# An attention and expert kernel with idle products at its start, seven logits, narrower scatters and new sequences

## The chip, the cores and the metric

The kernel runs on one core of a Trainium2 chip. The metric is the device time of one execution in microseconds. In the profile PE is TensorE, PEld its weight loads, DVE is VectorE, ACT is ScalarE, POOL is GpSimd and SP is SyncE, whose queue issues nearly all DMAs.

## The reference

Four batches of 12288 tokens of 128 numbers attend to 768 keys, which are means over 4 x 4 patches of `kv` times a matrix. What comes out goes, token by token, to the one of eight experts that has the largest logit.

```python
kv_pool = kv.reshape(B, H // r, r, W // r, r, C).mean(axis=(2, 4))
kv_flat = kv_pool.reshape(B, -1, C) @ w_sr
k = v = kv_flat
a = softmax(q @ k.transpose(0, 2, 1) / sqrt(C))      # rows of 768
x = (a @ v).reshape(B * N, C)
logits = x @ w_gate                                  # 8 experts
expert_idx = argmax(logits, axis=1)
gate_w = softmax(logits)[arange(N), expert_idx]
y = relu(x @ w1[expert_idx]) @ w2[expert_idx]        # 128 -> 1024 -> 128
out = gate_w[:, None] * y
```

## The kernel before

The tokens are worked on in 96 blocks of 512, 24 to a batch. For each batch `keys` first sums patches: twelve loads of `kv` are added in pairs on DVE (L604), and PE sums the rest and turns it by products with a unit matrix (`ident`), eight to a pair of loads. Projections with `w_sr` follow, then `expert` fetches the weights of the expert that the batch's mean points to, orders its hidden units and keeps 384 of them. The permutations that do this are written by comparisons (`PU`, L960).

A block computes scores (`s`) of 512 queries against six tiles of 128 keys, subtracts the exponential (ACT, `e`) from its linear part (DVE, `r`), and multiplies `r` with a tile of values: 24 products, four chunks of tokens by six tiles of keys, `XW` = 145 columns wide, to which a correction of 136 columns is added three times for each chunk. The columns behind the first 128 hold eight logits, the row sum, and eight sums over bands of keys by which tokens that lie badly are found. A first-guess expert serves all tokens of a batch. `group` and `marks` compare the logits, and tokens for which the guess fails are listed. A `general_step` per batch (three of them inside the schedule, after batches 0 to 2) fetches such tokens' values, works them out with their own expert and writes them over the results by a scatter on POOL (L1674). What is left over then goes through a loop at the end.

A block's hidden units come in three parts of 128. The third part has a flag by block (the ways named `u`): with it a sum is taken along by ACT and PE leaves out the last four products of that block; the blocks 14, 22, 37, 39 and 95 had no such flag.

The order is not left to a compiler. Each piece of work is an `op` of a class `Plan`, with engine, estimated time, what it needs and gives, and buffers. A table `ORDER` gives each engine its own sequence, a table `WAYS` picks between forms of a piece, and `order` walks both and starts what can start first. PSUM has two banks of the kind `b`, two double banks `s` and one `po`. Where PE would stand still in given stretches of the planner's time, the planner puts in idle products (`fill`): three products of 128 by 384 of the constant `slots16`, into a bank `b` that nobody reads. The constants are written by DVE and POOL ahead of the plan, in a schedule of their own.

Of the kernel before, what the change touches and what calls it, by code (L numbers as in the profile page):

```python
# [9 lines left out]
F32 = mybir.dt.float32  # L10
F16 = mybir.dt.float16
# [73 lines left out]
PE 0-2 4-5 3 6-7 9-10 8 11 112 13 114 12 100 16 101 115 14 113 103 15 147 17-18 102 23 119 117 146 118 116 19 105 148 104  # L85
107 106 125 124 151 150 149 126 152 135 24 136 26 20 129-130 128 137 127 157 25 31 159 141 139-140 138 21 158 32 168 22 169
161 160 162-163 30 170 28 181 27 29 180 121 173 179 120 172 174 171 108 191 131-132 190 185 182-183 192 122 184 123 133 212
201 195 110 134 109 203 194 153 193 155 196 154 202 111 213 142 214 206 143 207 223 164 205 224 204 33 144 236 145 225 216
165 218 217 234 215 34 186 235 156 245 227 188 187 229 226 228 246-247 208 166 238 240 239 237 257 175 35 258 248-249 36 256
197 189 251 176 268 177 250 37 267 167 178 262 269 260 198 259 209 261 278 199 210 280 270 200 272 220 273 279 219 271 211  # L90
39 291 283 290 282 231 281 284 221 289 230 38 300 222 301 40 42 41 294 232 293 292 302 241 295 313 243 233 312 252 304 242
306 253 311 46 305 324 263 303 47 323 43 317 48 244 322 265 314 316 315 254-255 49 333 328 326 264 276 327 335 44 274 325
334 275 266 346 285 344 45 339 287 337 345 307 277 355 286 336 338 296 298 357 356 297 350 348-349 347 381 288 380 308 360
309 361 359 401 358 299 52 390 379 50 53 392 318 383 403 385 329 402 319 382 51 384 391 310 412 406 320 407 413 330 321 414
362 404 341 405 331 425 340 332 423 393 363 396 364 395 394 424 343 415 418 435 417 416 434 386 351 436 426-427 429 54 428
445 55 365 352 446 438 342 439 447 437 387 366 440 456 397 388 458 449 353 450 457 448 451 354 469 467 398 389 408 468 461
399 419 479 460 367 459 410 462 409 480 430 400 478 421 473 470-472 420 500 411 501 56 482 431 57 370 483 452 489 432 491
# [4 lines left out]
591 600 70 612 593 66 532 611 553 610 71 602-603 605 551 604 552 72 622 621 562 543 613 623 614 632 563-564 616 615 554 633  # L102
573 634 565 67 656 575 626-627 624 574 625 658 68 657 584 636 638 667 585 635 637 576 689 76 668 662 659 586 661 660 595 691
669 75 73 587 596 690 671 607 673 672 670 606 712 617 74 695 678 597-598 680 693 608 679 692 619 694 700 639 609 701 683 618
682 702 628 684 630 681 629 713 620 722 703 641 640 705-706 711 77 643 734 704 78 631 724 642 723 675 714 716-717 664 715
663 733 665 735 674 685 725 727 644 726 745 676 728 666 744 687 737 739 746 738 707 696 736 677 766 747 697-698 768 749 748
686 750 767 718 79 647 699 778 645 777 770 80 769 646 709 779 771 729 772 708 688 719 757 756 782 720 710 783 755 731 780
648 781 649 730 789 760 759 721 650 741 790 758 761 788 651 799 740 654 801 652 791 800 732 793-794 792 810 751 81 811 802
82 804 812 773 753 803 805 653 834 83 833 742 815 813 752 814 743 821 774 816 822 655 823 762 832 754 775 843 824 784 826
844 763 85 827 845 825 776 84 856 835 855 786 838 837 86 854 764 836 88 87 846 785 848 867 849 795 847 765 866 92 876 858  # L110
796 860 797 857 859 865 787 798 877 888 808 93 806 819 89 807 868 878 871 869-870 818 887 817 889 94 881 880 809 900 879 95
898 882 840 820 893 899 829 892 90 828 891 890 91 830 911 910 839 850 904 831 933 901 903 852 934 902 842 97 909 935 841 96
98 956 912 862 913 851 915 914 99 863 944 957 936 853 861 938 955 883 939 872 937 946 873 864 894 966 874 961 884 945 875
# [8 lines left out]
1063 1147 1106 1165 1167 1116 1064 1180 1117 1179 1154 1181 1118 1108 1182 1138 1128 1153 1155 1119 1170 1129 1168 1127 1150
1169 1171 1183 1190 1151 1188 1149 1130 1156-1157 1140 1159 1139 1189 1152 1164 1158 1174 1141 1184 1192 1185 1194 1172-1173
1191 1193 1186-1187 1175 1160 1195 1161-1162 1197 1196 1200 1198 1163 1199 1201
ACT 0 2 1 3-4 6 5 7 113 9 115 8 104 10 105 116 11 114 107 12-13 139 20 19 14-15 106 138 117-118 140 108 123 109 122 22 124
130 21 142 141 23 131 16-17 132 18 125 146 126 24 148 29 133 147 154 30 155 149 28 156 150 26 164 25 134 27 163 120 162 119
158 157 110 172 128 171 127 173 121 165-166 129 185 112 178 111 180 167 143 145 174 179 144 186 135 187 136 193 151 194 31
181 204 137 195 152 202 32 189 188 203 168 210 170 169 196-197 212 211 153 182 206 205 218 33 219 159 34 217 175 198 160-161
# [226 lines left out]
def attention_moe(ctx: ExitStack, tc, q, kv, w_sr, w_gate, w1, w2, out):  # L355
# [43 lines left out]
    with tc.manual_schedule():  # L399
# [68 lines left out]
        for t in con:  # L468
            nc.vector.memset(t, 0.0)
# [1282 lines left out]
```

## Time and profile before

| | us |
|---|---|
| median of three runs | 727.38 |
| lowest and highest run | 727.12, 729.40 |
| the profiled execution's own time | 728.98 |
| its span | 727.2 |
| PE busy | 695.8 |
| DVE busy | 632.3 |
| ACT busy | 609.2 |
| POOL busy | 538.4 |

The span counts from the first to the last instruction; 1.78 us of the profiled execution lie around it. Busy times are those of the engine itself; register, branch and DMA-issuing instructions are not counted. The times in the views below are from the start of that span. The chain that ended last is followed from the last instruction back, at each step to what released it or to the instruction ahead of it on its engine.

### The profile page before, as it was taken

The page shows a single profiled execution, that of the slowest core. Times are in us where ns is not written, and L with a number is a line of the kernel's source. Part 1 is how long each engine was busy: PE and PEld are TensorE (multiplying, and loading weights), DVE is VectorE, ACT ScalarE, POOL GpSimd, SP SyncE. Part 2 cuts the span into 40 slices and gives each one's busy share as a digit, 9 for nine tenths or more (in the row PEclk, how much of TensorE's full clock was granted, in tenths as well). Part 3 has the DMA queues.
Part 4 walks back from the last instruction along what each step waited for, and adds up shares of the span by engine and source line. Part 5 has one row for each costly group of instructions (what it writes and reads, how often), then busy time and mean ns, then how long its engine had stood idle before and what let it go on. Part 6 is the DMA issues. An engine that isn't in the chain of part 4 may idle for free.

```text
span 727.2 us, 20777 instructions
## 1 busy us (share of the span) xinstructions
PE 695.8 (96%) x7874; PEld 548.7 (75%) x7874; DVE 632.3 (87%) x1262; ACT 609.2 (84%) x1120; POOL 538.4 (74%) x770
## 2 busy tenths in 40 slices
PE   4998999999999999999999999999999999999995
PEld 4676777888778767887687777888877877877774
DVE  5789888889998989789999898898998899778875
ACT  0578899899898988889878888899988898898973
POOL 0455899886888879686778978888778778657643
PEclk9999999999999999999999999999999999999999
DMA  8795987995999999878999999879886798985842
GB/s 336 186 271 116 248 200 185 196 211 127 202 250 243 229 232 216 198 175 136 184 211 209 230 218 275 167 146 211 156 170 152 175 186 195 195 154 117 130 91 74
DMA packets 324389, 138.25 MB, mean 190 GB/s; under 512 B 210190, under 2 KB 315794, under 8 KB 324288
## 3 DMA queue, kind: packets, MB, share of 16 engines
q1 hardware_dynamic: 323536, 136.55, 85.6%
q8 instruction: 62, 1.02, 0.6%
q14 instruction: 39, 0.32, 0.1%
q10 hardware_dynamic: 560, 0.20, 0.1%
q0 software_dynamic: 192, 0.17, 0.1%
HBM read 59.12 MB, written 26.94 MB: 118 GB/s over the span
## 4 chain that ended last, share of the span: by engine, by line
PE 71%; DVE 13%; ACT 7%; issue 4%; DMA 3%; POOL 1%; SPq 0%; DVEq 0%; ACTq 0%; POOLq 0%
PE b L478 31%; PE po L478 22%; PE s L478 16%; DVE r L1189 6%; ACT e L1187 3%; DMA kv<-in_kv_dram 2%; DVE y L1318 1%; DMA x<-xp 1%; ACT g L1293 1%; ACT X L1281 1%; DVE xp L1224 1%; ACT xp L1223 0%; DVE junk L1428 0%; PE s L859 0%; PE s L1588 0%
## 5 line engine op out<-in xcount | busy, mean ns | idle before, releaser
L1189 DVE SCALAR_TENSOR_TENSOR r<-s,e 128x1024 bf16<-128x1024 f32 x288 | 346.4, 1216 | 34.9 <-ACT e L1187 33.0
L1187 ACT ACTIVATE e<-s 128x1024 f32<-128x1024 f32 x288 | 294.2, 1031 | 35.6 <-PE s L478 29.8
L478 PE MATMUL po<-v,r 128*128 128x145 f16 x2304 | 252.9, 227 | 1.0 <-ACT lg L1231 0.8
L478 PEld LDWEIGHTS <-r 128*128 128x128 bf16 x2304 | 167.7, 98 | 21.6 <-DVE xp L1224 1.3
L478 PE MATMUL s<-qT,KT 128*128 128x512 f16 x576 | 168.0, 379 | 2.4 <-DVE r L1189 1.4
L478 PE MATMUL b<-x,w1U 128*128 128x512 f16 x465 | 142.5, 379 | 5.0 <-DMA x<-xp 1.5
L1293 ACT ACTIVATE g<-b,zb 128x512 f16<-128x512 f32 x187 | 129.3, 694 | 11.5 <-PE b L478 10.9
L478 PE MATMUL po<-M,qT 128*128 128x136 f16 x1152 | 130.9, 223 | 0.0
L1285 POOL TENSOR_TENSOR g<-X,g 80x512 f16<-80x512 f32 x94 | 108.8, 1157 | 29.1 <-ACT g L1293 9.5
L478 PE MATMUL b<-w2U,g 128*128 128x128 f16 x1172 | 128.3, 219 | 1.3 <-POOL g L1285 1.3
L478 PE MATMUL b<-L,x 128*128 128x128 f16 x1116 | 122.9, 219 | 0.1
L1170 POOL TENSOR_TENSOR qp<-qr,qp 128x512 f16<-128x512 f32 x94 | 108.8, 1160 | 8.5 <-DVE w1l L1012 1.2
L478 PEld LDWEIGHTS <-qT 128*128 128x128 f16 x1152 | 84.5, 98 | 28.1 <-issue 3.1
L478 PEld LDWEIGHTS <-x 128*128 128x128 f16 x1116 | 80.8, 98 | 16.8 <-issue 3.2
L1168 POOL CAST qp<-qr 128x512 f16<-128x512 f32 x94 | 57.2, 613 | 41.2 <-DMA qr<-in_q_dram 21.1
L1283 POOL CAST g<-X 128x512 f16<-128x512 f32 x94 | 58.2, 620 | 36.3 <-ACT X L1281 18.3
L478 PEld LDWEIGHTS <-g 128*128 128x128 f16 x1172 | 81.6, 98 | 1.4 <-POOL g L1285 1.4
L619 POOL TENSOR_TENSOR kv<-kv,kv 128x512 f32<-128x512 f32 x54 | 68.2, 1273 | 12.8 <-DVE sg L873 2.2
L478 PEld LDWEIGHTS <-w1U 128*128 128x128 f16 x480 | 45.7, 98 | 38.2 <-issue 4.2
L1281 ACT ACTIVATE X<-b,zb 128x512 f32<-128x512 f32 x94 | 65.1, 696 | 9.6 <-PE b L478 9.5
L1318 DVE TENSOR_TENSOR y<-b,gt 128x512 f32<-128x512 f32 (+1 forms) x97 | 65.3, 676 | 6.8 <-PE b L478 5.0
L478 PEld LDWEIGHTS <-KT 128*128 128x128 bf16 x576 | 51.0, 99 | 25.7 <-issue 4.6
(386 smaller groups left out, 912.0 us busy)
## 6 DMA issues: line engine op xcount, KB each, us to landing
qr<-in_q_dram SPq DMA_DIRECT2D x96, 256.0 KB, 3.6
out_dram<-y SPq DMA_DIRECT2D x95, 256.0 KB, 3.3
kv<-in_kv_dram SPq DMA_DIRECT2D x41, 512.0 KB, 6.0
raw<-in_moe_w_dram SPq DMA_DIRECT2D x14, 512.0 KB, 5.5
e<-in_kv_dram SPq DMA_DIRECT2D x3, 512.0 KB, 8.8
v_dram<-vT SPq DMA_DIRECT2D x4, 384.0 KB, 3.9
qT<-qp SPq DMA_TRANSPOSE x94, 3.7
x<-xp SPq DMA_TRANSPOSE x91, 3.6
```

The costliest lines, as they stand in the source:

```text
L478: return nc.tensor.matmul(o, l, r, start=start, stop=stop)
L619: nc.gpsimd.tensor_add(flat(to), flat(to), flat(of))
L1168: op("POOL", .62, lambda: nc.gpsimd.tensor_copy(qp.tile[:, 0], qr.tile), T - 1.9 * LEN, [("qr", t)], [("qh", t)], [qr, qp])
L1170: op("POOL", 1.17, lambda: nc.gpsimd.tensor_sub(qp.tile[:, 1], qr.tile, qp.tile[:, 0]), T - 1.8 * LEN, [("qh", t)], [("qp", t)], [qr, qp])
L1187: op("ACT", 1.03, lambda e=e, ps=ps: nc.scalar.activation(e.tile, ps.tile, AF.Exp), at + .6, [("s", t, s)], [("e", t, s)], [ps, e])
L1189: op("DVE", 1.22, lambda e=e, ps=ps, s=s: nc.vector.scalar_tensor_tensor(r.tile[:, 2 * s:2 * s + 2], ps.tile, 1.0, e.tile, op0=ALU.add, op ...
L1224: op("DVE", .69, lambda: nc.vector.tensor_tensor(xp.tile[:, 1], po.tile[:, :, :C], xp.tile[:, 0], op=ALU.subtract), A + .5, [("xh", t)], [ ...
L1281: op("ACT", .69, lambda ph=ph, zu=zu: nc.scalar.activation(gf.tile, ph.tile, AF.Relu, bias=zu()), at + .5, [("ph", t, u), ("zb", b)], [("g ...
L1283: op("POOL", .62, lambda: nc.gpsimd.tensor_copy(gg.tile[:, 0], gf.tile), at + 1.5, [("gf", t)], [("gh", t), ("g", t)], [gf, gg])
L1285: op("POOL", 1.16, lambda: nc.gpsimd.tensor_sub(gg.tile[:PAIRS, 1], gf.tile[:PAIRS], gg.tile[:PAIRS, 0]), at + 2, [("gf", t), ("gh", t), ( ...
L1293: op("ACT", .78, lambda u=u, ph=ph, zu=zu: nc.scalar.activation(gg.tile[:, u], ph.tile, AF.Relu, bias=zu(), accum_out=k["fl"].tile[:, u - ...
L1318: nc.vector.tensor_tensor(y.tile[:, cs], py.tile.rearrange("p (c d) -> p c d", d=C)[:, cs], bc(gr["gt"].tile[:, 0, js], C)[:, cs], op=ALU. ...
```

## The change

- The logit of the first-guess expert is no longer carried: seven others (`EO = E - 1`) stand in the extra columns. `XW` becomes 144 and the correction 135 columns. `relative` and a new step `others` fill the gap with the eighth expert.
- The blocks 14, 37 and 39 take the way with a flag.
- The scatter of a general step names only the rows of the batches that are done (12288, 24576 and 36864 instead of 49152), and `v_dram` likewise.
- The two loads of expert weights in a general step are an operation of their own; in `expert` they are two.
- Idle products are allowed from 3.5 instead of 9.0 us of the planner's time. Their groups of three go from 11 to 20: 11 ahead of the first key sums, one among them and 8 later. Before, all 11 came after the key sums.
- Constants and plan share one schedule.
- `ORDER` and `WAYS` are new: twelve of the 32 `PU` rows are written by POOL, tiles of `kt` and the first scaled weights leave DVE, and 18 instead of 20 blocks send `x` over POOL. Some new forms are written but not picked (`f`, `n`, `y`).

```diff
-PE 0-2 4-5 3 6-7 9-10 8 11 112 13 114 12 100 16 101 115 14 113 103 15 147 17-18 102 23 119 117 146 118 116 19 105 148 104
...
-            if o.eng == "PE" and any(lo < free["PE"] and start < hi for lo, hi in self.filler_times):
+            spans = [lo for lo, hi in self.filler_times if lo < start and free["PE"] < hi] if o.eng == "PE" else ()
+            if spans:
                 make, fill, us = self.filler
+                free["PE"] = max(free["PE"], spans[0])
...
-    XW = C + NG + 1 + E
+    EO = E - 1
+    XW = C + EO + 1 + NG
...
-    with tc.manual_schedule():
-        ident = keep("ident", [P, P])
...
+    written = ExitStack()
+    written.enter_context(tc.manual_schedule())
+    ident = keep("ident", [P, P])
...
-        op("DVE", .8, unit, at + 2, [("pd", b), ("mean", b)], [("unit", b)], [pd])
+        op("DVE", .87, unit, at + 2, [("pd", b), ("mean", b)], [("unit", b)], [pd])
...
+            op("ACT", .2 + .21 * w, lambda sl=sl: nc.scalar.activation(
+                kt.tile[:, sl], vT.tile[:, sl], AF.Identity, bias=cn[:, :1], scale=cn[:, 4:5]), at + 2.1 + n,
+               [("unit", b), ("vT", b)], [("kt", b), ("kt", b, n)], [vT, kt], way=(f"t{b}{n}", 1))
...
+        def others():
+            c = cg.tile
+            nc.vector.scalar_tensor_tensor(c[:, 0, :EO], c[:, 1, :EO], c[:, 0, EO:], c[:, 0, :EO], op0=ALU.mult, op1=ALU.add)
+            nc.vector.tensor_scalar(c[:, 4, 1:2], cn[:, 12:13], -1.0, -1.0, op0=ALU.mult, op1=ALU.add)
+            nc.vector.scalar_tensor_tensor(c[:, 2, :EO], c[:, 1, :EO], c[:, 4, 1:2], iota_e[:, :EO], op0=ALU.mult, op1=ALU.add)
...
+        op("DVE", .7, others, at + 12, [("cg", b)], [("off", b)], [cg], lock=True)
...
+            if way:
+                op("POOL", .5, lambda j=j: nc.gpsimd.tensor_scalar(
+                    PU.tile[:, j], slots16, sg.tile[:, 8, j:j + 1], 1.0, op0=ALU.is_equal, op1=ALU.mult),
+                   at + 22 + j / 2, [("odd", b)], [("perm", b, j)], [PU, sg], way=(way, 1))
...
-                            mm(po.tile[:, c, :P + E], own_q(c, i), M.tile[:, j], False, False)
...
+                            mm(po.tile[:, c, :P + EO], own_q(c, i), M.tile[:, j], False, False)
...
-        part("SP", 2.3, load, ["find"], "load", [gi, vT, *raw], 4.5, moves=4.2)
+        part("SP", 1.1, load, ["find"], "load", [gi, vT], 4.0, moves=1.0)
+        part("SP", 1.6, load_w, ["find"], "loadw", [gi, *raw], 4.5, moves=3.4)
...
-            out=out, out_offset=bass.IndirectOffsetOnAxis(ap=li(4), axis=0),
-            in_=o.tile, in_offset=None, bounds_check=B * N - 1, oob_is_err=False), ["o"], "done", [gi, o], 2.5)
+            out=out[:upto * N], out_offset=bass.IndirectOffsetOnAxis(ap=li(4), axis=0),
+            in_=o.tile, in_offset=None, bounds_check=upto * N - 1, oob_is_err=False), ["o"], "done", [gi, o], 2.5)
...
-            op("DVE", .8, count_steps, START + (t + 5) * LEN + 3, [("left", b)], [("steps", b)], lock=True)
+            op("DVE", .8, count_steps, START + (t + 5) * LEN + 3,
+               [("left", b)] + [("general", b - 1, "find2")] * (b - 1 in STEPS_AFTER), [("steps", b)], lock=True)
...
-    plan.filler, plan.filler_times = (bank().make, fill, .487), ((9.0, 110.0), (690.0, 800.0))
-    with tc.manual_schedule():
-        plan.issue()
+    plan.filler, plan.filler_times = (bank().make, fill, .487), ((3.5, 110.0), (690.0, 800.0))
+    plan.issue()
+    written.close()
```

On PE the program began with the product of the gate weights' maximum (`b0_166`) and the first key sums; a name is the tile with a running number, behind it the operands and the shape, and in brackets the engines waited for.

```order
L478 MATMUL b0_166<-wg_st_95,ones_72 128x1 [waits DVE_49]
L478 MATMUL s0_208<-ident_65,kv3_176 128x128 [waits DVE_49,Pool_49]
L478 MATMUL s0_208<-ident_65,kv3_176 128x128 x7
L478 MATMUL s0_208<-ident_65,kv2_174 128x128 x8
L478 MATMUL s1_226<-ident_65,kv4_180 128x128 [waits DVE_49]
```

Now the idle groups stand between them; the first, the second and the last of the eleven:

```order
L483 MATMUL b0_161<-wg_st_95,ones_72 128x1 [waits DVE_49]
L483 LDWEIGHTS slots16_86
L483 MATMUL b1_194<-slots16_86 128x384
...
L483 MATMUL b1_198<-slots16_86 128x384 [waits PE_49]
...
L483 MATMUL b1_234<-slots16_86 128x384 [waits PE_49]
...
L483 MATMUL s0_238<-ident_65,kv2_167 128x128 [waits DVE_49,Pool_49]
L483 MATMUL s0_238<-ident_65,kv2_167 128x128 x7
```

All eleven groups go to the bank `b1`, and each but the first waits for PE itself, for the group ahead of it in that bank; `b0_161` holds the other bank.

On DVE the reduction of the gate weights (L514, now L519) was the first instruction, and the last constants stood among the key additions:

```order
L514 TENSOR_REDUCE wg_st<-wg_raw 128x1
L403 CAST ident_h<-ident 128x128
...
L452 TENSOR_SCALAR band_i<-part_i 128x1
L604 TENSOR_TENSOR kv_174<-kv_174,kv_164 128x1024
L453 CAST band<-band_i 128x1
L604 TENSOR_TENSOR kv_176<-kv_176,kv_172 128x1024
```

Now it is behind all of them:

```order
L470 MEMSET ends 128x65
L474 MEMSET con_143 128x32
...
L519 TENSOR_REDUCE wg_st<-wg_raw 128x1
L609 TENSOR_TENSOR kv_167<-kv_167,kv_165 128x1024
L609 TENSOR_TENSOR kv_169<-kv_169,kv_163 128x1024
L486 TENSOR_SCALAR wg_st<-b_161 128x1
```

All constants have moved ahead of the reduction, and the reader of the product of the gate weights (L486) behind two key additions.

On POOL the scatter of the first general step stood ahead of casts and subtractions of hidden units, and waited for two DMA queues:

```order
L995 TENSOR_SCALAR sg_6038<-sg_6038,ws_6196 128x8 [waits Pool_49]
L1674 DMA out_dram<-pool_5680,gi_4611 49152x128 [waits DMAHW5_49,DMAHW0_49]
L1283 CAST g_6086<-X_6265 128x512 [waits Activation_49]
L1229 TENSOR_TENSOR xp_6182<-X_6148,xp_6182 128x512 [waits DVE_49]
L1283 CAST g_6185<-X_6164 128x512 [waits PE_49]
L1285 TENSOR_TENSOR g_6086<-X_6265,g_6086 80x512 [waits Pool_49]
```

Now it waits for none:

```order
L1219 TENSOR_TENSOR qp_5725<-qr_5544,qp_5725 128x512 [waits DVE_49]
L1727 DMA out_dram<-pool_5710,gi_4680 12288x128
L1334 TENSOR_TENSOR g_5995<-X_5910,g_5995 80x512 [waits DVE_49,Activation_49,Pool_49]
L1406 TENSOR_TENSOR gt_5864<-gt_5864 128x16
L1407 TENSOR_SCALAR gt_5864<-gt_5864,con_144 128x16 [waits Pool_49]
```

The waits for stores are gone from it, and its neighbours are others.

On SP the three loads of that general step were neighbours:

```order
L1517 DMA gk_4655<-v_dram 128x768 [waits DMAHW7_49]
L1518 TENSOR_LOAD gi_4611
L1518 ISA x2
L1519 ISA
L1519 DMA raw_4656<-in_moe_w_dram 128x1024 [waits DMAHW0_49]
L1520 ISA
L1520 DMA raw_4657<-in_moe_w_dram 128x8x128 [waits DMAHW1_49]
L1248 DMA_TRANSPOSE x_4741<-xp_4475 128x8x128 [waits DMAHW2_49,Pool_49]
```

Now the values' load stands alone:

```order
L1567 DMA gk_4698<-v_dram 128x768 [waits DMAHW7_49]
L1372 DMA out_dram<-y_4739 128x4x128 [waits DMAHW0_49,DVE_49]
L551 DMA kv_4761<-in_kv_dram 128x1x1024 [waits DMAHW1_49]
L1297 DMA_TRANSPOSE x_4774<-xp_4349 128x8x128 [waits DMAHW2_49]
L1203 DMA qr_4829<-in_q_dram 128x4x128 [waits DMAHW3_49,Pool_49]
```

The two loads of weights have moved some fifteen rows further down.

## Rows read from the trace of the kernel before

**Rows 1.** The page: busy us (share) by engine; the last chain by engine.

```profile
PE 695.8 (96%) x7874; PEld 548.7 (75%) x7874; DVE 632.3 (87%) x1262; ACT 609.2 (84%) x1120; POOL 538.4 (74%) x770
...
PE 71%; DVE 13%; ACT 7%; issue 4%; DMA 3%; POOL 1%; SPq 0%; DVEq 0%; ACTq 0%; POOLq 0%
```

**Rows 2.** By stretch: length, each engine's busy us (count), PE clock, DMA.

```profile
0.00:11.20 11.20, 0.59 (x2) 0.50 (x2) 5.65 (x37) 1.28 (x1) 1.35 (x10) 1.00 0.81 298
11.20:24.40 13.20, 13.12 (x93) 12.70 (x94) 7.94 (x23) 2.00 (x7) 2.33 (x3) 1.00 0.92 311
24.40:46.00 21.60, 19.65 (x156) 13.46 (x155) 18.08 (x46) 17.03 (x30) 11.41 (x15) 1.00 0.85 260
...
100.00:700.00 600.00, 592.82 (x6841) 468.64 (x6839) 535.12 (x1006) 531.01 (x977) 471.57 (x656) 1.00 0.90 190
254.00:268.00 14.00, 12.38 (x135) 9.19 (x132) 11.36 (x27) 11.38 (x23) 11.03 (x17) 1.00 0.96 212
338.00:354.00 16.00, 14.23 (x149) 10.82 (x147) 15.44 (x22) 14.13 (x21) 9.66 (x19) 1.00 0.72 136
```

**Rows 3.** The same view, PE's products into the s banks, at the start.

```profile
13.24:15.24 2.00, 2.00 (x12) 1.00 1.04 389
15.60:17.60 2.00, 2.00 (x20) 1.00 1.05 387
```

**Rows 4.** Timeline of PE, start: start, us, work, count, [idle before].

```profile
2.85 0.59 PE L478 MATMUL b<-wg_st,ones 128*128 128x1 f32 x2 [2.85 <-DVE ones L405]
11.24 7.65 PE L478 MATMUL s<-ident,kv 128*128 128x128 f32 x48 [7.80 <-DVE band L455]
18.72 1.95 PE L478 MATMUL s<-ident,e 128*128 128x128 f32 x16
...
34.89 1.14 PE L478 MATMUL b<-slots 128*128 128x384 f16 x6
```

**Rows 5.** Chain that ended last, start: start, us, what.

```profile
24.89 0.50 PE b L478 x2
...
32.01 0.66 PE b L478 x3
32.67 0.04 issue
```

**Rows 6.** Timeline of DVE at the start, columns as in rows 4.

```profile
2.36 0.16 DVE L514 TENSOR_REDUCE wg_st<-wg_raw 128x1 f32<-128x8 f32 x1 [2.36 <-DMA wg_raw<-in_moe_w_gate_dram]
2.44 0.22 DVE L403 CAST ident_h<-ident 128x128 f16<-128x128 f32 x1
...
5.41 0.10 DVE L452 TENSOR_SCALAR band_i<-part_i 128x1 int32<-128x1 int32 x1
...
9.76 0.15 DVE L453 CAST band<-band_i 128x1 f32<-128x1 int32 x1
...
16.40 0.21 DVE L469 MEMSET con<- 128x32 f32 x4
...
20.47 0.69 DVE L566 TENSOR_TENSOR r<-r,r 128x512 f32<-128x512 f32 x1 [0.71 <-DMA r<-in_kv_dram]
```

**Rows 7.** The chain late in the span, columns as in rows 5.

```profile
680.30 0.86 PE s L478 x4
...
689.31 1.34 PE b L478 x24
```

**Rows 8.** Timeline of POOL at the end of batch 0's general step.

```profile
342.28 1.10 POOL L1674 DMA_INDIRECT out_dram<-pool,gi  x1 [3.11 <-DMA out_dram<-y]
```

**Rows 9.** Timeline of PE in the two stretches with idle time.

```profile
264.70 0.82 PE L478 MATMUL b<-x,w1U 128*128 128x512 f16 x3 [1.46 <-DMA x<-xp]
...
346.85 0.29 PE L478 MATMUL b<-w2U,g 128*128 128x128 f16 x2 [1.25 <-POOL g L1285]
```

**Rows 10.** Timeline of SP's queue at the start of that general step.

```profile
257.49 4.59 SPq L1248 DMA_TRANSPOSE x<-xp  x1
```

**Rows 11.** DVE's writes of PU: count, min/median/max ns, first and last start.

```profile
L960 DVE TENSOR_SCALAR PU<-slots,sg x32: 301/314/807, 71.3 to 538.7; 128x384 f16<-128x384 f16 x32
```

More of the change, by code (lines that the diff above doesn't have):

```diff
@@ L89 @@
[L89 to L93, printed above, removed]
@@ L122 @@
[L122 to L126, printed above, removed]
@@ new lines, in attention_moe @@
+    part_col = keep("part", [P, 1])
+    nc.vector.tensor_copy(part_col, part_i)
+    own = keep("own", [P, UH + OWN])
+    nc.vector.memset(own, 0.0)
+    for i in range(OWN):
+        nc.vector.tensor_scalar(own[:, UH + i:UH + i + 1], part_col, float(OWN_AT + i), None, op0=ALU.is_equal)
+        nc.vector.scalar_tensor_tensor(own[:, OWN_U:OWN_U + 1], own[:, UH + i:UH + i + 1], OWN_ONE, own[:, OWN_U:OWN_U + 1],
+                                       op0=ALU.mult, op1=ALU.add)
+    rare = keep("rare", [P, P])
@@ new lines, in attention_moe @@
+    nc.vector.tensor_copy(band, band_i)
+    band1 = keep("band1", [P, 1])
+    nc.vector.tensor_scalar_add(band1, band, 1.0)
+    for t in range(KT):
+        nc.vector.tensor_scalar(extra[:, t, 1:], slots16[:, :NG], band1, -1.0, op0=ALU.is_equal, op1=ALU.mult)
+    below = keep("below", [P, P])
+    nc.vector.tensor_scalar(below, slot[:, :P], part_col, None, op0=ALU.is_gt)
+    below_b = keep("below_b", [P, P], BF16)
+    nc.vector.tensor_copy(below_b, below)
+    step = keep("step", [P, 1])
@@ L477, in mm @@
+    nc.vector.memset(step, 0.0)
+    ends = keep("ends", [P, NL + 1])
+    nc.vector.memset(ends, FAR)
+    n_left = keep("n_left", [P, 1], I32)
+    con = [keep(f"con{b}", [P, 32]) for b in range(B)]
+    for t in con:
+        nc.vector.memset(t, 0.0)
+    first_i = [keep(f"first{b}", [P, 1], I32) for b in range(B)]
+    v_dram = dram.tile([B, P, NK], F32, name="v_dram")
+    nc.scalar.dma_start(wg_raw, w_gate)
+    nc.scalar.dma_start(wsr, w_sr)
     def mm(o, l, r, start, stop):
@@ L613, in keys, with four, add_all @@
                     op("PE", 1.75, add, at + 6 + i, [("two", b, d, i)] + [("pt", b, d, i - 1)] * (i > 0),
-                       [("pt", b, d, i + 1)], [pt, raw])
+                       [("pt", b, d, i + 1)], [pt, raw], way=(f"f{d}", 0))
+                def four(raws=raws):
+                    flat = lambda t: t.tile.rearrange("p a j c -> p (a j c)")
+                    nc.vector.tensor_tensor(flat(raws[0]), flat(raws[0]), flat(raws[2]), op=ALU.add)
+                def add_all(raw=raws[0], pt=pt):
+                    for j in range(POOL):
+                        for a in range(2):
+                            mm(pt.tile[:, a, :P], raw.tile[:, a, j], ident, j == 0, j == POOL - 1)
+                op("DVE", 1.22, four, at + 9, [("two", b, d, 0), ("two", b, d, 2)], [("four", b, d)], [raws[0], raws[2]], lock=True,
+                   way=(f"f{d}", 1))
+                op("PE", 1.75, add_all, at + 10, [("four", b, d)], [("pt", b, d, 3)], [pt, raws[0]], way=(f"f{d}", 1))
                 turned = lambda pt=pt: pt.tile[:, :, :P]
@@ L906, in expert, with count @@
             junk = buf("junk", [P, F], BF16)
+            way = f"n{b}" if j else None
             op("ACT", 1.25, lambda j=j, junk=junk: nc.scalar.activation(
                 junk.tile, krow.tile, AF.Sign, bias=key(j), scale=-1.0, accum_out=lc(j)), at + 13.5 + j, [("krow", b)],
-               [("less", b, j)], [krow, sg, la, junk])
+               [("less", b, j)], [krow, sg, la, junk], way=(way, 0) if way else None)
+            def count(j=j, junk=junk):
+                nc.vector.tensor_scalar(junk.tile, krow.tile, key(j), None, op0=ALU.is_lt, op1=ALU.add, accum_out=lc(j))
+                nc.vector.tensor_scalar(lc(j), lc(j), 2.0, float(1 - F), op0=ALU.mult, op1=ALU.add)
+            if way:
+                op("DVE", 1.35, count, at + 13.5 + j, [("krow", b)], [("less", b, j)], [krow, sg, la, junk], lock=True,
+                   way=(way, 1))
         def chosen(j):
```

448 lines of the change are left out of this document (223 added, 225 removed), and 34 rows, old and new, of the table ORDER.

## The prediction

> **What bounds the kernel now.** I read the page's busy shares and its chain first, then the table by stretches, then the start and the two ends of a batch instruction by instruction. TensorE (PE) is busy 96% of the span, and the chain that ended last lies on it for the greater part [rows 1]. The table [rows 2] tells where the other 4% are. Between 100 and 700 us PE is busy 592.82 of 600 us, so there a PE instruction that goes is worth its whole time and nothing on VectorE (DVE), ScalarE (ACT) or GpSimd (POOL), which all have slack, is worth anything unless PE waits for it. PE's 7.2 us of idle in that middle are the most that better sequences can bring there; the stretches 254 to 268 and 338 to 354 alone hold 1.62 and 1.77 of them. At the start PE does 0.59 us of work in the first 11.2 us, then is busy all through (13.12 of 13.20) until 24.4, then idles 1.95 us up to 46.
>
> The start has a second loss. The clock column shows 1.00 throughout, but the products tell another pace: 12 key sums in 2.00 us at 13.24 and 20 of the same shape in 2.00 us at 15.60 [rows 3]. So PE runs the first of them at the lower of its two levels (1.2 GHz) and goes to the upper one (2.4 GHz) after it has worked from 11.24 [rows 4] to about 15.4. All 48 sums of the first pass take 7.65 us; sixteen at the upper level take 1.95 [rows 4].
>
> **Part 1, fewer logits.** A row of values is 144 instead of 145 columns wide and its correction 135 instead of 136. That is 96 blocks x 4 x 6 = 2304 and 1152 products with one column less, 3456 columns. The price of a column comes from two rows late in the chain: 4 products of 512 columns in 0.86 us are 215 ns each, 24 of 128 columns in 1.34 us are 55.8 ns each [rows 7], so (215 - 55.8) / 384 = 0.415 ns a column. 3456 x 0.415 = **-1.43 us**, all on PE and nearly all in the stretch where PE is the bound. The small DVE steps that the seven logits need (three more per batch) hide in DVE's slack; uncovered they would be about 0.2 us each, 2.4 in all.
>
> On this the Trainium skill speaks against the change: "TensorE: Matmul & The Clock Gate", section "Back-to-back issue gap", has the spacing of a stream of weight load and product set by both, 81 ns at 128 columns, by which a column less would be worth nothing. The 55.8 ns of this trace lie well below that; the rule is kept as a rival.
>
> **Part 2, flags.** Blocks 14, 37 and 39 now take the way that leaves out four products of 128 columns each: 12 x 55.8 ns = **-0.67 us** on PE. In exchange ACT writes a sum in three activations, under its slack.
>
> **Part 3, scatters.** POOL's first scatter waits 3.11 us for stores of `out` [rows 8]. Behind it in POOL's queue stand the casts and subtractions of hidden units, and PE then waits 1.25 us for one of these subtractions [rows 9]. In the changed kernel that scatter names the rows of batch 0 only and has no wait for stores left. I take those 1.25 us off. The bounds: 0, if the subtraction is late anyway, and 1.77, all idle of that stretch [rows 2]. **-1.25 us.** Stores that stood behind the scatter on SyncE (SP) go out earlier too, which nothing on PE is waiting for.
>
> **Part 4, weights of the general step.** At 257.49 a transposition of `x` follows three loads in SP's queue and takes 4.59 us [rows 10]; PE waits 1.46 us for an `x` there [rows 9]. The changed order puts two large loads eight places and more away. I take **-1.0 us**, with bounds of 0 (the transposition is held by something else) and -1.46.
>
> **Part 5, the start.** Three things follow one another.
> (a) When can the idle products begin? Their PE queue place is behind the product of the gate weights, which needs DVE's reduction, which now stands behind all constants. Before, that reduction was DVE's first work, at 2.36; the constants ran from 2.44 to 5.51 with four steps of the gate weights between them, and eight further kinds, 2.06 us in sum, filled gaps from 9.76 to 16.40 [rows 6]. In one piece that is some 2.7 + 2.06 us, then 0.16 for the reduction and about half of the 0.59 for the product [rows 4], 5.3 in all. If DVE begins at 1.4 the idle products start at 6.6; with a start at 2.44 as before, or waits between dependent small steps, at 7.9. I take 6.9.
> (b) How long do 11 groups of three take? With both banks, two groups last 1.14 us [rows 4]; in one bank each waits for the one before, 0.70 from start to start (0.66 and 0.04) [rows 5]. In the changed order all eleven are in one bank, since the other one holds the product of the gate weights, whose reader on DVE stands behind two key additions. At the lower level a group costs between 0.97 and 1.41; I take 1.2. Letting the first products run slow for as long as the sums did, 3.5 groups cost 4.2 us and 7.5 cost 5.25: the first sum starts at 6.9 + 9.45 = **16.35**, against 11.24. Bounds: 14.4 (6.6 and all at 0.70) and 20.1 (all at 1.2).
> (c) What is it worth? From 11.24 to the last projection of the keys at 24.89 [rows 5] are 13.65 us. At the upper level the 48 sums take some 5.4 instead of 7.65, a gain of 2.2; one idle group among the sums costs 0.3. So that projection comes at 16.35 + 11.75 = 28.1: **+3.2 us** on the path. The data do not cover it: the last key addition is done at 21.16 [rows 6], well ahead of the sums then. Bounds: +1.3 and +7.0.
>
> **Part 6, after the key sums.** Eight idle groups instead of eleven, and three times 0.66 on the chain [rows 5] is 2.0; PE's idle up to 46 us is 1.95 [rows 2], some of it for DVE steps that have moved to ACT or POOL. So between 0 and -3.9; I take **-1.5**, since idle groups partly stand where PE waits in any case. The permutations that move to POOL later (12 of 32, 0.30 us each on DVE [rows 11]) lie under slack and count nothing; uncovered they are 3.6 us.
>
> Sum: -1.43 - 0.67 - 1.25 - 1.0 + 3.2 - 1.5 = -2.65 us. The profiled execution took 728.98 us (727.2 span and 1.78 around it) and lies 1.60 above the median, so it would come to 726.3, and the median of 727.38 to **724.7 us**.
>
> **The rivals.**
> Slower: the lower level holds through all idle products. For it: these are the first work of PE and sit with a wait between every two groups; against it: the sums, the first work of PE before, were slow only to about 15.4, and they too had waits for data between them. The first sum then starts at 20.1, the start costs +7.0, and nothing comes back afterwards: 727.4 - 1.43 - 0.67 - 1.25 - 1.0 + 7.0 = 730.0. It decides from a first sum at about 19.7.
> Same: the new sequences change every queue, and waits like those of parts 3 and 4 return at other places; PE's idle in the middle stays at 7 us. For it: these waits fall where a long queue meets a rare event, and every batch has such events. Then the 2.25 of parts 3 and 4 are lost: 727.0.
> Earlier: the idle products run at two banks' pace and at the upper level from the first: 6.6 + 11 x 0.49 = 12.0, the start gains 1.1 and the sum is 720.4. Against it stands the one bank.
> Columns worth nothing: the weight load ahead of each product, 128 columns whatever the product's width, sets the pace of the values, and part 1 vanishes: 724.7 + 1.4 = 726.2. Against it stand the 24 products of 1.34 us, each behind a load of its own. This is the rule of the Trainium skill that part 1 cites.
>
> **How the numbers follow.** This kernel's measurement tells 0.3% (2.2 us) from no change: faster is below 725.2, slower above 729.6. The forecast's case gets 0.48, of which 0.08 end above 725.2 (a first sum at 17 or later, or parts 3 and 6 at half); the earlier start 0.08; the waits elsewhere 0.27; the columns worth nothing 0.02; the slow start 0.15. So faster 0.48, same 0.37, slower 0.15. The range runs from 720.5, where the bounds of parts 3, 4 and 6 meet the earlier start, to 729.2, which leaves most of the slow start out.
>
> **What would show it.** The first key sum of the changed kernel at 14.4 to 20.1, at 20 in 2.00 us from the first one on (part 5); idle groups 0.70 apart with a slow stretch first; POOL's first scatter with no wait before it and no PE wait of over 1 us behind it (part 3); no `x` that PE waits for over 1 us near the first general step (part 4); PE idle between 100 and 700 us below 6. It is wrong if the first sum starts before 13, if waits of 2 us or more appear between 100 and 700, or if DVE or POOL, not PE, is the one that others wait for after 46 us.

## The result: 0.7% slower, and the profile after

The changed kernel takes 733.29 us (median of five runs, 732.74 to 735.35). The kernel before, with runs on the same chips added, takes 729.0 (five runs). The ratio is 1.0066, with a 95% interval of 1.0038 to 1.0093. The forecast was 724.7 us, that is faster; the range ended at 729.2. The profiled execution of the changed kernel took 732.74 us, its span is 731.0, 3.8 us more than before.

The same table by stretches as [rows 2], of the changed kernel, with one more stretch at the end, which is where the answer lies:

```profile
0.00:11.20 11.20, 4.48 (x16) 2.05 (x17) 6.31 (x47) 1.28 (x1) 1.28 (x9) 1.00 0.80 299
11.20:24.40 13.20, 12.82 (x93) 10.14 (x92) 6.96 (x13) 1.39 (x5) 0.00 (x0) 1.00 0.93 310
24.40:46.00 21.60, 19.29 (x149) 13.61 (x148) 16.66 (x48) 16.50 (x32) 11.30 (x18) 1.00 0.71 214
...
100.00:700.00 600.00, 590.87 (x6808) 467.17 (x6807) 526.72 (x1002) 532.33 (x987) 480.76 (x664) 1.00 0.87 190
254.00:268.00 14.00, 13.86 (x162) 10.88 (x160) 13.08 (x35) 13.04 (x27) 10.19 (x15) 1.00 0.87 211
338.00:354.00 16.00, 15.90 (x165) 11.97 (x163) 15.45 (x25) 15.95 (x27) 11.80 (x20) 1.00 0.77 152
525.00:550.00 25.00, 20.63 (x214) 15.23 (x213) 18.32 (x35) 16.88 (x34) 19.40 (x23) 0.93 0.62 115
```

and the last of these stretches of the kernel before:

```profile
525.00:550.00 25.00, 24.96 (x307) 19.67 (x305) 22.25 (x47) 21.98 (x43) 18.18 (x27) 1.00 0.85 171
```

The two stretches that held the idle time before are full now: PE's idle fell from 1.62 to 0.14 and from 1.77 to 0.10 us. Yet between 100 and 700 us PE idles 9.13 us instead of 7.18, since 525 to 550 alone has 4.37 of it, 0.04 before, and there the clock column falls below 1.00 as well. Counted by PE over the whole span: idle time 30.1 instead of 31.4 us, busy time 700.9 instead of 695.8. So the span is 3.8 us longer with PE idle less: the idle products are 60 instead of 33, and 3.4 us of work ran at the lower clock level. That count hides the waits. Most of the new idle products fill the first 11.2 us, where PE is busy 4.48 instead of 0.59 us; in the rest of the span its idle time has grown by 2.6 us.

The timeline of PE around the place (start, busy us, line, work, [idle before]):

```profile
537.33 0.33 PE L483 MATMUL b<-L,x 128*128 128x128 f16 x3
540.60 0.28 PE L483 MATMUL b<-w2U,g 128*128 128x128 f16 x2 [2.95 <-POOL g L1332]
541.84 0.23 PE L483 MATMUL b<-w2U,g 128*128 128x128 f16 x1 [0.95 <-POOL g L1334]
```

POOL's timeline there shows what stood ahead of the cast (L1332) and the subtraction (L1334) that PE waits for:

```profile
531.37 3.13 POOL L1007 TENSOR_SCALAR PU<-slots,sg 128x384 f16<-128x384 f16 x2
534.48 0.42 POOL L1389 TENSOR_TENSOR lg<-lg,cg 128x112 f32<-128x112 f32 x1
534.98 0.38 POOL L1395 TENSOR_TENSOR gd<-lg,gt 128x112 f32<-128x112 f32 x1
535.33 4.66 POOL L1007 TENSOR_SCALAR PU<-slots,sg 128x384 f16<-128x384 f16 x3
539.94 0.61 POOL L1332 CAST g<-X 128x512 f16<-128x512 f32 x1
540.63 1.15 POOL L1334 TENSOR_TENSOR g<-X,g 80x512 f16<-80x512 f32 x1
```

These are rows of `PU` of batch 3, which the change gave to POOL. By instruction (count, min/median/max ns):

```profile
L1003 DVE TENSOR_SCALAR PU<-slots,sg x20: 305/470/1001, 73.6 to 533.0; 128x384 f16<-128x384 f16 x20
L1007 POOL TENSOR_SCALAR PU<-slots,sg x12: 1557/1580/1590, 73.3 to 541.9; 128x384 f16<-128x384 f16 x12
```

One costs 1.58 us on POOL and cost 0.31 on DVE [rows 11]; the planner's entry for it is 0.5. Behind the two waits PE runs at the lower level, as the clock column (the third from the end) of a stretch of 3.40 us shows:

```profile
542.40:545.80 3.40, 3.40 (x26) 2.51 (x23) 2.61 (x3) 0.81 (x2) 3.30 (x7) 0.51 0.00 0
```

Half of 3.4 is 1.7 us; with 2.95 and 0.95 that makes 5.6 us for this one place as a first estimate, more than the whole 3.8.

### The profile page after: what moved, and what is told of

Read it like the earlier page. It is cut to its first block, busy times and chain, and to the rows that moved or that the text cites. A ratio compares the mean times of both kernels' runs of the same rounds, so it can differ in the third digit from the quotient of the medians.

```text
span 731.0 us, 20831 instructions
## 1 busy us (share of the span) xinstructions
PE 700.9 (96%) x7889; PEld 549.3 (75%) x7889; DVE 626.5 (86%) x1260; ACT 612.1 (84%) x1130; POOL 551.2 (75%) x779
## 4 chain that ended last, share of the span: by engine, by line
PE 71%; DVE 12%; ACT 8%; POOL 4%; issue 3%; DMA 1%; ACTq 0%; POOLq 0%; DVEq 0%
PE b L483 33%; PE po L483 22%; PE s L483 15%; DVE r L1238 5%; ACT e L1236 4%; POOL PU L1007 1%; ACT g L1342 1%; DVE xp L1273 1%; DMA qT<-qp 1%; DVE y L1367 1%; POOL g L1334 1%; PE s L1641 1%; ACT xp L1272 0%; DVE PU L1003 0%; DVE w2l L1066 0%
## 5 line engine op out<-in xcount | busy, mean ns | idle before, releaser
L483 PE MATMUL po<-v,r 128*128 128x144 f16 x2304 | 251.5, 226 | 0.7 <-DVE r L1238 0.3
L1342 ACT ACTIVATE g<-b,zb 128x512 f16<-128x512 f32 x190 | 131.5, 693 | 10.7 <-PE b L483 8.2
L483 PE MATMUL po<-M,qT 128*128 128x135 f16 x1152 | 131.9, 223 | 0.0
L1334 POOL TENSOR_TENSOR g<-X,g 80x512 f16<-80x512 f32 x94 | 108.7, 1157 | 27.6 <-ACT g L1342 15.0
L1332 POOL CAST g<-X 128x512 f16<-128x512 f32 x94 | 57.4, 611 | 29.3 <-ACT X L1330 4.7
```

Source lines behind the costliest of these rows:

```text
L483: return nc.tensor.matmul(o, l, r, start=start, stop=stop)
L1332: op("POOL", .62, lambda: nc.gpsimd.tensor_copy(gg.tile[:, 0], gf.tile), at + 1.5, [("gf", t)], [("gh", t), ("g", t)], [gf, gg])
L1334: op("POOL", 1.16, lambda: nc.gpsimd.tensor_sub(gg.tile[:PAIRS, 1], gf.tile[:PAIRS], gg.tile[:PAIRS, 0]), at + 2, [("gf", t), ("gh", t), ( ...
L1342: op("ACT", .78, lambda u=u, ph=ph, zu=zu: nc.scalar.activation(gg.tile[:, u], ph.tile, AF.Relu, bias=zu(), accum_out=k["fl"].tile[:, u - ...
```

## The experiments

Theory A: the six `PU` products (the comparisons that write `PU`) of batch 3 on POOL cost the 5.6 us, and the start a further part. The rivals are named with each run. Times are medians; where a ratio is given it is to the kernel before on the same chip, with its 95% interval.

### The suspect taken back

```diff
-... p24 p27 d2 t30 p32 p33 p34 p35 p36 p37 d3 ...
+... p24 p27 d2 t30 d3 ...
```

`ORDER` was carried over; the six stand on DVE behind the two `PU` products of that batch which were there.

> The changed kernel with the six PU products of batch 3 back on DVE (behind its other two), nothing else. Theory A: on POOL each takes 1.58 us, six of them stand ahead of a cast and a subtraction of hidden units, PE then idles 2.95 and 0.95 us at 537 to 542 and runs at the lower clock level for the 3.4 us after it (about 1.7 us lost). Expected by A: 733.3 - 5.6 = 727.7 us, no PE wait over 1 us between 525 and 550, no stretch at the lower level before the end. Rival B: the late subtraction comes from the order of POOL's queue as such, and another wait takes its place: 731.5 or more, with a PE wait of over 1.5 us near the same place.

Measured: 728.12 us, 0.9992 (0.9977 to 1.0007). That is 5.2 us below the changed kernel, and the stretch is full again, at full clock (stretch as above):

```profile
525.00:550.00 25.00, 24.45 (x280) 18.39 (x279) 22.70 (x48) 22.24 (x43) 15.50 (x24) 1.00 0.85 174
```

Theory A holds, rival B falls: no other wait took the place.

### The suspect alone, in the kernel before

```diff
+            if b == B - 1 and j >= 2:
+                op("POOL", .5, lambda j=j: nc.gpsimd.tensor_scalar(
+                    PU.tile[:, j], slots16, sg.tile[:, 8, j:j + 1], 1.0, op0=ALU.is_equal, op1=ALU.mult),
+                   at + 22 + j / 2, [("odd", b)], [("perm", b, j)], [PU, sg])
+                continue
```

> The kernel before with the six PU products of batch 3 on POOL (five ahead of block 64's cast and one behind its subtraction), nothing else: the suspected part alone. Theory A: PE waits 3 to 5 us for POOL near 535 to 545 and falls to the lower clock level after it: 729.5 + 5 to 6 = 735 us. Rival: the kernel before has room on POOL there and 731 us or less is measured.

Measured: 735.55 us, 1.0092 (1.0067 to 1.0117), 7 us more than before. The same waits appear, and two more behind them (PE's timeline):

```profile
540.08 0.28 PE L478 MATMUL b<-w2U,g 128*128 128x128 f16 x2 [2.29 <-POOL g L1288]
541.38 0.23 PE L478 MATMUL b<-w2U,g 128*128 128x128 f16 x1 [1.01 <-POOL g L1290]
542.92 0.49 PE L478 MATMUL b<-PU,w1l 128*128 128x128 f16 x6 [0.20 <-POOL PU L961]
546.45 1.46 PE L478 MATMUL b<-PU,w1h 128*128 128x384 f16 x8 [1.95 <-DVE y L1323]
```

So it is this edit, in either kernel's sequence. The clock stays at its upper level in this stretch, so that here the loss is waiting alone and that part of the expectation failed:

```profile
525.00:550.00 25.00, 19.51 (x224) 14.61 (x222) 16.42 (x30) 17.14 (x33) 21.78 (x24) 1.00 0.60 125
```

PE idles 5.49 us there, 0.04 in the kernel before. The 7 us hold something else as well: of the 7.2 us between the two profiled spans (734.4 and 727.2), 5.1 stand ahead of the start of the last product of values (713.4 against 708.3) and 2.1 behind it. There the clock column is 0.50 from 722 to 726 us with PE at work for 3.08 of the 4 us; in the kernel before it first falls behind PE's last product. So the six products cost nearer to 5 than to 7 us here too.

### Only the order of POOL's queue

In `ORDER` of POOL, the cast and the subtraction of block 64 go ahead of the last four `PU` products.

```diff
-... PU5 PU6 PU3 gh64 g64 see16 PU2 ...
+... gh64 g64 PU5 PU6 PU3 see16 PU2 ...
```

(The table has numbers; the names here are those of the operations.)

> The changed kernel with one cast and one subtraction of hidden units (block 64) put ahead of the last four of the six PU products in POOL's queue; POOL's work is the same. Rival B, the order of the queue alone costs the time: PE's waits of 2.95 and 0.95 us go, the lower clock level with them, and 728.5 us are left. Theory A, POOL has too much to do there with products of 1.58 us: PE waits for PU or for a later block's subtraction instead, 731 us or more.

Measured: 734.31 us, 1.0060 (1.0042 to 1.0077), as slow as the changed kernel. PE's list of waits in 100 to 700 us (line, releaser, us, times, longest) begins with

```profile
PE b L483 <- POOL PU L1007: 4.6, 1, 4.6
```

The wait has only changed its name: PE gets the hidden units in time and then waits 4.6 us for `PU`. In this run POOL works 9.4 us on the six, from 530.8 on, and PE asks for the last at 538.4, 7.6 us later; DVE finishes their input only at 530.4. Six products do not fit there, wherever the cast stands, as long as PE's own sequence stays.

### PE kept busy through the wait

```diff
             Lt, w = k["L"].tile, k["w2U"].tile
+            for _ in range(15 if t == 64 else 0):
+                mm(py.tile[:, :UN], slots16[:, :P], slots16, True, True)
```

> The changed kernel with fifteen idle products of PE put in where PE waits for POOL (ahead of block 64's outputs), 2.4 us of the 2.95 us wait. Theory A splits the loss into 3.9 us of waiting and 1.7 us of the lower level behind it; with PE busy the level stays and only the waiting is paid: 733.3 - 1.7 = 731.6 us. Rival: the level falls all the same, or the idle products come on top: 733.3 us or more.

Measured: 732.39 us, 1.0055 (1.0035 to 1.0074), 0.9 below the changed kernel, which the intervals don't separate. The clock stays at its upper level in the same 3.40 us:

```profile
542.40:545.80 3.40, 2.66 (x27) 1.74 (x25) 2.61 (x4) 1.29 (x2) 3.30 (x7) 1.00 0.02 5
```

but PE is busy only 2.66 of them. What the faster clock saves is in part waited again, for POOL's last `PU` and for DVE (PE's timeline):

```profile
543.44 0.49 PE L483 MATMUL b<-PU,w1l 128*128 128x128 f16 x6 [0.38 <-POOL PU L1007]
544.73 1.46 PE L483 MATMUL b<-PU,w1h 128*128 128x384 f16 x8 [0.36 <-DVE y L1369]
```

The same product behind the place, in the changed kernel, in this run and in the first run, with the six on DVE:

```profile
546.74 0.38 PE L483 MATMUL b<-x,w1U 128*128 128x512 f16 x1
546.02 0.38 PE L483 MATMUL b<-x,w1U 128*128 128x512 f16 x1
541.10 0.38 PE L483 MATMUL b<-x,w1U 128*128 128x512 f16 x1
```

The last products ahead of the place (two `s<-qT,KT`) begin at 536.89, 536.77 and 536.80. From there it is 9.85, 9.25 and 4.30 us: the six on POOL do cost 5.6 us here, but the slow clock is only 0.6 of it. So the split into 3.9 of waiting and 1.7 of slow clock is right as a reading of the rows, and wrong as a price list.

### The start without idle products ahead

```diff
-((3.5, 110.0), (690.0, 800.0))
+((20.0, 110.0), (690.0, 800.0))
```

> The changed kernel without the eleven groups of idle products ahead of the key sums (the nine later ones stay). Theory A: the groups delay the first key sum from 11.2 to 15.7 us and give back 2.2 us of it by the upper clock level. Expected by A: first sum at 11.2, twelve or fewer sums in the first 2 us, the last projection of the keys at 25 to 25.5, and 733.3 - 2.8 = 730.5 us. Rival C: the start is made up later in any case, because a DMA or DVE sets the pace of the first blocks: 733 us, with block 3 as late as in the changed kernel.

Measured: 732.40 us, 1.0049 (1.0031 to 1.0067), 0.9 below the changed kernel, which the intervals don't separate. The start is as expected, the keys' last projection begins at 25.11 instead of 27.75:

```profile
11.20 7.41 PE L483 MATMUL s<-ident,kv 128*128 128x128 f32 x48 [4.12 <-DVE kv L609]
...
25.11 0.46 PE L483 MATMUL b<-pT,wsr 128*128 128x128 f32 x2
```

Of the 2.64 us gained there 0.9 shows in the time (1.2 by the two ratios), and none in the profiled span (732.1 against 731.0). In the profiled run of this kernel the clock fell once more, behind a chain of short waits in batch 0 (0.88, 0.31, 0.38 and 0.62 us between 61 and 69 us):

```profile
69.70:73.00 3.30, 3.30 (x19) 2.57 (x20) 3.27 (x9) 0.98 (x3) 3.03 (x6) 0.50 0.93 270
```

and a wait for an `x`, which the changed kernel does not have, stands in the list of PE's waits:

```profile
PE b L483 <- DMA x<-xp: 1.0, 1, 1.0
```

### Four groups ahead instead of eleven

```diff
-                    if at + us > start:
+                    if at + us > start or 5.7 < at < 20.0:
```

> The changed kernel with four groups of idle products ahead of the key sums instead of eleven. Theory A: they end near 10.8, the first sum starts at 11.2 to 11.4 and all sums run at the upper level, so that PE waits for DVE's additions and the last projection comes at 23 to 23.7: 733.3 - 4.5 = 728.8 us. Rival D: PE falls back to the lower level in the waits between sums and nothing but the delay is regained: 730.5 us.

Measured: 730.73 us, 1.0012 (0.9993 to 1.0032), 2.6 below the changed kernel (3.9 by the two ratios). The first sum comes at 11.38, all sums run fast, and the last projection begins at 23.48, 4.27 earlier than in the changed kernel:

```profile
6.94 4.64 PE L483 MATMUL b<-slots 128*128 128x384 f16 x12
11.38 5.61 PE L483 MATMUL s<-ident,kv 128*128 128x128 f32 x48
...
23.48 0.46 PE L483 MATMUL b<-pT,wsr 128*128 128x128 f32 x2
```

So the first idle products do buy the clock, and the seven groups behind them buy nothing. Of the 4.27 only 2.0 are left in the profiled span (729.0 against 731.0), and PE idles 11.6 instead of 9.1 us between 100 and 700: the largest loss on the way is a wait for a transposed query,

```profile
433.15 0.60 PE L483 MATMUL s<-qT,KT 128*128 128x512 f16 x2 [1.52 <-DMA qT<-qp]
```

which stands in neither kernel's list of waits. Rival D is wrong on the clock and right on the sum.

### The price of a column

The changed kernel with the values' products 160 instead of 144 columns wide; the added columns are constants that nobody reads.

```diff
-mm(po.tile[:, c, :XW], r.tile[:, kt, c * P:(c + 1) * P], v16.tile[:, kt, :XW], kt == 0, kt == KT - 1)
+mm(po.tile[:, c, :XW + 16], r.tile[:, kt, c * P:(c + 1) * P], v16.tile[:, kt, :XW + 16], kt == 0, kt == KT - 1)
```

> The changed kernel with 16 columns more in each of the 2304 products of values (filled with constants that nobody reads). Theory A, columns cost 0.415 ns each: 2304 x 16 x 0.415 = 15.3 us more, 748.6 us. Rival E, the weight load ahead of each product sets the pace and columns are worth nothing: 733.3 us.

Measured: 743.91 us, 10.6 above the changed kernel; by the page's first part PE's busy time goes from 700.9 to

```profile
PE 712.9 (96%) x7889; PEld 564.5 (76%) x7889; DVE 626.8 (85%) x1260; ACT 614.2 (83%) x1130; POOL 551.7 (75%) x779
```

A column costs 10.6 us / 36864 = 0.29 ns of time (some 0.2 to 0.4 by the intervals of the two ratios), 12.0 / 36864 = 0.33 of PE's busy time. That is not nothing (rival E falls), and it is less than 0.415.

### Two edits of the change alone, in the kernel before

The scatter's rows alone:

```diff
-            out=out, out_offset=
-            in_=o.tile, in_offset=None, bounds_check=B * N - 1,
+            out=out[:(B if n is None else n + 1) * N], out_offset=
+            in_=o.tile, in_offset=None, bounds_check=(B if n is None else n + 1) * N - 1,
```

> The kernel before with the scatter's rows limited to finished batches, nothing else. Expected by part 3 of the prediction: no wait of 3.1 us before POOL's first scatter, no wait of PE for the subtraction near 346.9, PE idle in 338 to 354 down from 1.77 to about 0.5 us. Rival: the scatter has no wait and the subtraction is late all the same, PE idle 1.5 or more.

Measured, a single time: 727.72 us, span 725.9; the kernel before took 727.09 to 732.37 on the same chip, so the time alone tells nothing. POOL's wait went from 3.11 to 0.50 us, PE's wait behind it is gone, and PE's idle in the stretch is 0.24 us (a row of POOL's timeline, and one of the table by stretches):

```profile
338.66 1.10 POOL L1674 DMA_INDIRECT out_dram<-pool,gi  x1 [0.50 <-issue]
```

```profile
338.00:354.00 16.00, 15.76 (x180) 12.66 (x179) 15.34 (x26) 15.88 (x25) 11.86 (x19) 1.00 1.02 159
```

The two loads of weights alone, sixteen places later in SP's queue:

```diff
-        part("SP", 2.3, load, ["find"], "load", [gi, vT, *raw], 4.5, moves=4.2)
+        part("SP", 1.1, load, ["find"], "load", [gi, vT], 4.0, moves=1.0)
+        part("SP", 1.6, load_w, ["find"], "loadw", [gi, *raw], 4.5, moves=3.4)
```

> The kernel before with the two loads of expert weights in the general step of batch 0 sixteen places further back in SP's queue, nothing else. Expected by part 4: no wait of PE for an x near 264.7 (1.46 us before), PE idle in 254 to 268 down from 1.62 to 0.2 to 0.6. Rival: x is late for another reason, PE idle 1.3 or more.

Measured, a single time: 732.21 us, span 730.3. The wait for `x` is gone and the stretch is nearly full, but the one behind it (the last row is that of the kernel before) has 1.57 us of idle instead of 0.68, and waits for `qT`, which the kernel before does not have, head PE's list of waits in 100 to 700 us:

```profile
254.00:268.00 14.00, 13.74 (x153) 10.36 (x151) 12.99 (x28) 13.02 (x25) 11.04 (x16) 1.00 0.82 185
268.00:338.00 70.00, 68.43 (x784) 55.84 (x782) 59.88 (x124) 59.14 (x111) 55.49 (x76) 1.00 0.92 202
268.00:338.00 70.00, 69.32 (x791) 56.36 (x789) 60.73 (x125) 59.84 (x114) 54.90 (x75) 1.00 0.92 196
```

```profile
PE s L478 <- DMA qT<-qp: 1.9, 3, 1.1
```

Part 4's edit alone, in the old sequence, moves the wait on: between 100 and 700 us PE idles 8.40 us, 7.18 before. The single time lies within the runs of the kernel before and can't tell a gain of a microsecond or two. How long PE waits for that `x` also varies without the edit: it is 0.8 us in the run with the scatter's rows alone.

### Both repairs, and POOL without any of the twelve

The first and the sixth edit together:

```diff
-... t30 p32 p33 p34 p35 p36 p37 d3 ...
+... t30 d3 ...
...
-                    if at + us > start:
+                    if at + us > start or 5.7 < at < 20.0:
```

> The changed kernel with both repairs: the six PU products of batch 3 on DVE, and four groups of idle products ahead of the key sums instead of eleven. Theory A, the two places are independent: 733.3 - 5.2 - 2.6 = 725.5 us, against 729.5 of the kernel before. Rival D: the four microseconds gained at the start are waited away at transpositions and loads in the middle, and 727.5 or more is left.

Measured: 725.31 us, 0.9929 (0.9907 to 0.9952). The two gains of 5.2 and 2.6 add up, as expected (725.5).

Then all twelve `PU` products on DVE, with the four groups:

```diff
-k1 k2 t00 t01 p03 p04 d0 t10 p12 p13 d1 t20 p24 p27 d2 t30 p32 p33 p34 p35 p36 p37 d3 ...
+k1 k2 t00 t01 d0 t10 d1 t20 d2 t30 d3 ...
```

> As e5 (both repairs), with the six PU products of batches 0 to 2 on DVE as well, so that POOL has none of the twelve. Theory A, what PU costs on POOL is the length of 1.58 us where POOL is short of time: batches 0 to 2 have two products each and no PE wait behind them, so 725.3 us within 1 us. Rival F, every PU product on POOL delays the blocks behind it: 723.5 us or less.

Measured: 722.73 us, 0.9916 (0.9897 to 0.9934). This beats both kernels. Its median is 2.6 us below that of the run above, where rival F would have it and theory A would not, but against the same chip's kernel before the two intervals overlap. Of the 1.5 us between the two profiled spans (723.6 and 722.1), 0.9 stand ahead of the first `PU` product: the first product of values starts at 41.4 and 40.5. So whether the two products each of batches 0 to 2 cost anything stays open.

## Why the prediction was wrong, point by point

- **The step that failed is the last sentence of part 6.** It took the twelve `PU` products at what DVE saves and gave POOL no price at all: "lie under slack and count nothing; uncovered they are 3.6 us". The trace of before has no such product on POOL, so it needed a bound from the nearest rows of POOL, and the names of what is queued behind. Those rows lie far apart. A subtraction of 80 by 512, as in the rows of POOL above, takes 1.15 us; by its columns that is 0.86 for 384 as an estimate, and six in one batch are over 5 us of POOL ahead of casts that PE needs. Nearer in kind is a multiplication with an addition, also a `tensor_scalar` (kernel before):

```profile
L695 POOL TENSOR_SCALAR KT<-vT,con x3: 902/907/907, 142.0 to 488.3; 128x768 bf16<-128x768 f32 x3
```

  By its columns that is 0.45 for 384, 2.7 us for six, which would have fitted. So the rows of before could have raised the question and could not answer it. It measured 1.58 each, and 5.2 us of time for six of them (5 to 7 in the kernel before). With this term the sum would have been 724.7 + 5.2 = 729.9, to which the 1.6 us come by which the median of the kernel before rose with more runs. Of the 1.8 us that are still missing, part 6 would be 1.5 and part 1 0.4; parts 3 to 5 missed by less than 0.5 each.
- **The shares hid it.** POOL's busy share of 74% over the span [rows 1] was read as slack everywhere. In 525 to 550 us POOL was busy 18.18 of 25 us before; 9.5 us more don't fit in the 6.8 that were free.
- **Part 5, the start, was right.** The idle products begin at 6.94 (6.9 was said), the first key sum at 15.73 (16.35), at the upper level by its pace (the clock column shows 1.00 at the start in every run), and the last projection at 27.75 instead of 24.89 [rows 5], +2.9 (+3.2). The eleven groups take 8.8 us up to the first sum (9.45). In PE's timeline of the changed kernel:

```profile
6.49 0.59 PE L483 MATMUL b<-wg_st,ones 128*128 128x1 f32 x2 [6.49 <-DVE wg_st L519]
6.94 8.96 PE L483 MATMUL b<-slots 128*128 128x384 f16 x33
15.73 5.52 PE L483 MATMUL s<-ident,kv 128*128 128x128 f32 x48
...
27.75 0.46 PE L483 MATMUL b<-pT,wsr 128*128 128x128 f32 x2
28.05 0.60 PE L1209 MATMUL b<-ident,qr 128*128 128x128 f32 x4
28.48 0.82 PE L736 MATMUL s<-ident,vT 128*128 128x128 f32 x6
29.73 0.61 PE L483 MATMUL s<-qT,KT 128*128 128x512 f16 x2 [0.43 <-ACT KT L710]
```

  What the prediction did not say is what the runs without seven or eleven of the groups show: 4.3 us at the start reach the end as 2.6, and 2.6 us as 0.9 (3.9 and 1.2 by the ratios). In their profiled runs, waits for transposed `qT` and `x` and short waits take part of it; how much they take on average is open.
- **Part 6, the gain of 1.5 behind the key sums, did not come.** Between 24.4 and 46 us PE idles 2.31 us where it idled 1.95, with eight groups of idle products there in either kernel; the three fewer of the sum are not on this path. The first product of values starts at 44.77 instead of 41.84 us, so the 2.9 us of the start are all still there. PE now waits for steps of ACT there: the last row above is such a wait of 0.43 us.
- **Parts 3 and 4 did what they should in the changed kernel**: 1.67 and 1.48 us less idle, where 1.25 and 1.0 were said. Part 3 does so alone as well. Part 4 does not: alone it only moves the wait. In the changed kernel it works together with the new sequences, and the runs don't separate the two.
- **Part 1 was too large.** A column is worth 0.29 ns in time, so 3456 of them 1.0 us, not 1.43. The price was taken from products that fill PE one after another. With the wider products PE's idle time over the span fell from 30.1 to 27.6 us, so part of the added work went into time in which PE would have waited; why its busy time also grew by less than 0.415 a column is open. The prediction read the Trainium skill's figure of 81 ns at 128 columns ("TensorE: Matmul & The Clock Gate", "Back-to-back issue gap") as a price of zero. The section's other figure, 131 ns at 512 columns, makes it 0.13 ns a column, an estimate from that page of the Trainium skill. The 10.6 us of the wider products speak against either here.
- **Part 2** (0.67 us) is below what a run can tell and was not tried alone.
- **The rivals.** The slower one that was written down (the lower clock level through all idle products) did not happen. The mechanism that did, a wait elsewhere, was the "same" rival, but with the size of the waits that the change removes as its price. Its true price was that of the operations which the change puts on another engine, and its own words, "the new sequences change every queue", should have led to the queue that got six new instructions of unknown length. The sign that was set for it, a wait of 2 us or more between 100 and 700 us, did come: 2.95 us for POOL.

The ledger of the two profiled spans: the start +2.9, `PU` +5.6, together 8.5 of which 3.8 are left; so all else brought -4.7. Of these, PE's idle between 100 and 700 us outside 525 to 550 is 2.4 (7.14 to 4.76), the columns by the run's price 1.0, the flags by the prediction 0.7; 0.6 is not assigned. In time, 2.6 of the start came back with four groups, 0.9 with none, which is not clear of nothing, and 5.2 of `PU`.

## What to carry to other kernels

An operation that moves to another engine is priced on that engine, from its own rows there, and in the stretch where it lands, not against the engine's share over the span. Where it has no row there, the nearest rows give a range at best (0.45 to 0.86 us here for what took 1.58), and a run with the operation alone is needed. A queue that gets several such operations right ahead of work that TensorE waits for is the first place to look, and reordering that queue does not help when the operations themselves don't fit between input and use. Idle products pay only until the clock has risen: here four groups were enough, and seven more pushed the first sum back by 4.35 us, of which 2.6 reached the end.

## What the runs showed of the hardware that was not expected

- The same comparison of 128 by 384 f16 takes 0.31 us on DVE (median in the kernel before) and 1.58 us on POOL, where a multiplication by one stands behind it: five times as much, with little spread (1.557 to 1.590). Two operations alone do not make it: the multiplication with an addition of 128 by 768 above takes 0.91 us on POOL. What does is open.
- Two waits of PE of 2.95 and 0.95 us, with 0.3 us of work between them, were followed by 3.4 us at 1.2 GHz in the changed kernel; fifteen idle products in the first of them kept 2.4 GHz, and in the kernel before with the same `PU` products two waits of 2.29 and 1.01 us were not followed by a lower level. In the run without idle products ahead, four waits of 0.88, 0.31, 0.38 and 0.62 us were followed by it; in the changed kernel the same four, of 0.88, 0.30, 0.36 and 0.62, were not. So of like waits some cost the clock and others do not.
- The 3.4 us at 1.2 GHz cost 0.6 us of time in that place, not 1.7: at 2.4 GHz PE waited again, for POOL and for DVE.
